# A fused attention and gated long convolution: last attention output through the DMA crossbar, biases by full-row products, smaller masks, another order

## Chip, cores and metric

The kernel runs on one core of a Trainium2 chip. The core has a matrix engine (PE, with its weight loads shown as PEld), a vector engine (DVE), an activation engine (ACT), GpSimd (POOL) and SyncE (SP); SP and POOL are used here mainly to issue DMAs. Every engine works through its own list of instructions in order, and waits there for semaphores of others. The metric is the device time of one execution in microseconds (us), the median of several runs.

## The reference

Four batches of eight heads, 768 positions, head size 64. The attention keeps, for each query, the eight first keys and the 96 keys up to itself, with a penalty that grows with distance, a slope for each head. Its output is the input `x` of a gated convolution over the whole sequence, done by Fourier transform.

```python
scores = scale * q @ k^T                                  # scale = 1/8
rel = pos[:, None] - pos[None, :]
is_global = pos[None, :] < 8;  is_local = (rel >= 0) & (rel < 96)
dist = where(is_global & ~is_local, 96, abs(rel))
scores = scores - slopes[h] * dist                        # slopes[h] = 2 ** -(h+1)
a = softmax(where(is_global | is_local, scores, -1e9));   o = a @ v
x = o.transpose(0, 2, 1, 3).reshape(4, 768, 512)
x1, x2, x3 = split(x @ w_proj, 3)                         # 512 -> 3 * 512
y = x1 * irfft(rfft(x2) * rfft(filter_fft)) * x3
out = y @ w_out                                           # float32, (4, 768, 512)
```

## The kernel before

**Attention.** Keys are cut into seven tiles `m` of 128 rows: the eight global keys first, then 120 keys of their own. A key tile meets 216 queries (168 and 48 in the last two). `attention(b)` works in three groups `c` of key tiles, (0, 1), (2, 3), (4, 5, 6). For each group, q and k tiles are transposed to `QT` and `KT` (by PE products with an identity, `turned`, or for batch 0's first tiles from f32, `turned32`; for batch 3 by transposing DMAs that SP issues, `crossed`). `scores` makes, for a pair of heads `hp`, two PSUM banks of 432 columns, ACT takes the exponential of both into `E` (L721), and DVE multiplies with `mask`, the exponential of the penalties (L738). In batch 0 there is no such product: the penalties are added to the scores in PSUM, by products of 64 rows with the tables `near` and `slope` (L698). `values` (L756, L761) multiplies with v and a column of ones, `rc` (L785) takes the reciprocal of the sums, and the product with it (L780) gives `xn`. `transpose_x` (L801) turns `xn` on PE, and a copy (L303) puts it into `xT`.

**Gates and convolution.** `gate` makes x1 and x3 for 384 positions at a time from `xT` (L840); x1 is scaled out of PSUM (L307, L309), x3 is copied out by ACT (L849) and multiplied by x1 on DVE (L851), or DVE takes x3 from PSUM in that product. `butterfly` adds and subtracts the halves and thirds of the sequence (L816 to L827); `conv` projects them (L909, evicted to `ab`), transforms (`forward`, L621, evicted to `X`), multiplies with the filter's spectrum (L1061 to L1078), transforms back (`inv`, L934, evicted to `eo`), joins the thirds and halves (`mixed`, `gated`; L1018 to L1041, the last one the product `y*g` with the gate), multiplies with `w_out` (L961), evicts to one of six tiles `ot` and stores.

**Tables.** In the beginning `setup`, `distances`, `masks`, `tables`, `inverse_tables` and `spectrum` make identities, penalties, masks, the Fourier matrices (from angles, with the sine on ACT), and the filter's spectrum.

**Loads.** SP brings four f32 tiles at first (`load_first32`); POOL issues all other loads of q, k, v, the weights and the filter, and casts them to 16 bit (L319). The first eight keys and values of a batch are copied to all tiles by further DMAs that SP issues (`kglobal`, `vglobal`).

**The order.** The program is a list of operations (`Plan.op`). Which engine does each, in which order, and in which PSUM banks, is written out in the text `ORDER`: `738V` is operation 738 on DVE, `31A` on ACT, `87P0` on PE into bank 0, G is POOL and S is SP. `i14b0` are 14 products of zeros into bank 0. An operation's number is its place in the order in which the functions list them. No cost decides anything at run time; the engines follow this list and their semaphores.

```python
n = next(i for i, x in enumerate(word) if x in "PAVGS")
o, at = self.ops[int(word[:n])], [int(x) for x in word[n + 1:]]
o.eng = word[n]
```

Of the kernel before, what the change touches and what calls it, by code (L numbers as in the profile page):

```python
# [16 lines left out]
P = 128  # L17
NG = 8
# [21 lines left out]
5G 33V 34A 1V 16S 0V 12V 20S 4V 41A 43A 9V 8V 39A 10A 44A 36A 6A 49A 48A 19S 37A 45A 24G 17S 18S 50G 55G 25V 11V 26G  # L40
13V 56G 40A 42A 7V i14b0 87P0 54G 28A 53G 60G 31A 85P1 61G 59G 27A 72V 62G 52G 35A 81P2 51G 57G 46A 58G 83P3 47A 88A
29V 30V 32V 90P0 63G 89A 86A 82V 38A 91V 84A 21V 114P2 115V 94P01 98P45 116P2 78A 65G 99A 64G 15V 117V 95A 92P67 112P3
113V 93A 110P2 96P45 97A 158P3 66G 111V 122P01 123A 120P67 121A 22V 68G 159V 3G 160P3 161V 14V 23S 156P2 118P45 162P3
67G 119A 124P01 261G 157V 163V 164P23 125A 166P45 100P01 165A 101V 102V 167A 105P67 170P23 171A 69G 168P01 169A 131P45
262G 263G 106V 107V 108P2 132V 133V 260G 126P67 127V 76A 103P3 104A 109V 128V 75A 134P4 221P5 74A 135V 172P01 73A 173V
259G 129P6 216P4 177P23 79A 130V 136P6 174V 175P7 178V 70G 146P0 217A 264S 179V 180P1 137P2 222A 223V 142P3 176A 218V
219V 71G 80A 271G 202V 181A 183P1 182P4 203V 220A 224V 209V 144A 141P5 210V 138A 211V 148V 205V 361P3 273G 225A 139V
140V 272G 270G 265S 188P7 185A 362A 212V 213V 151P6 266G 363P3 2A 153V 143A 364V 359P2 360V 152P6 228P3 154V 276G
365P01 190A 184V 77A 204V 279G 366A 206V 207V 371P45 198P2 277G 226V 367V 155V 297P7 368P01 214V 372A 373V 215V 208V
200A 374P45 187P6 278G 229A 274G 145V 491G 298A 288P2 375A 269G 275G 369A 289A 488G 286P7 227V 235V 236V 189V 237V  # L50
147P4 149V 238V 287A 150V 230A 231A 232A 233V 284P2 285A 312P7 292P6 313A 293A 389P5 387P2 192P7 390A 194A 193P6 195A
388V 394P45 395A 400P01 234V 391P23 392A 239V 240V 376V 299P7 300A 437P6 401A 301P4 302A 282G 268S 433P5 435P7 438V
281G 370V 397P23 398A 241V 249P6 250A 393V 434V 247P4 436V 402V 267S 382P01 494S 242P5 248A 448P67 243A 439P23 493S
440A 383V 384V 449A 396V 303P4 377P01 197P5 199A 304A 399V 408P23 441V 492G 244P6 378V 379V 305P5 409V 410V 380P4
445P01 245A 442P23 280G 381V 306A 196V 446A 450V 403P67 404V 443A 411P5 489G 587P4 499G 405V 256P01 412A 490G 385P6
257A 505G 386A 258A 591P7 588V 252P45 253A 254A 507G 406P0 447V 456P23 661P1 444V 508G 501G 662A 407V 414P0 589P4 590A
251V 307V 416A 310P5 311A 511G 290P6 424P1 457V 458V 291A 426A 459P0 423P4 425A 429P6 308V 431A 500G 451P23 665P1
418P6 255V 592A 191V 615P4 314V 315V 506G 718G 309V 322P7 452V 246A 460A 502G 420A 453V 186V 323A 617P5 719G 454P0
455A 295V 294V 296V 732G 666V 318P6 721S 413P7 616A 330P0 316P2 509G 481V 482V 484V 317A 326P1 618A 415A 663P4 428P2
201V 430V 319A 320P3 321V 324P5 483V 325A 331V 328P7 327A 419P6 329A 421V 422V 495G 472P2 730G 664A 283G 734G 466P7  # L60
432V 476P3 474A 497S 468A 599P45 735G 628P01 478V 600A 498G 529P2 332V 629A 485V 486V 530A 462P3 676P45 677A 333V 601V
673P01 674A 596P67 487V 516P2 597A 334V 464A 512P4 726G 513A 527P5 602P67 517V 717G 593P23 603A 630V 728G 619P01 620A
525P4 675V 514P6 528V 335V 336V 339V 504G 526A 622P01 496S 594A 625P45 626A 340V 477P7 621V 623A 479A 627V 598V 515A
503G 737G 427V 467P2 469A 350P3 670P01 739G 624V 667P45 671A 540P7 541A 604V 353P6 722S 716G 533P2 668A 733G 595V 337V
461P0 354A 520P7 470V 531P1 605P45 417V 606V 521A 729G 351A 818S 538P6 607V 534A 356P7 539A 817S 636P45 338V 463A 637V
532A 638V 631P23 632V 357A 633A 518P0 471P1 639P7 640A 519A 672V 473A 669V 678V 341P6 342A 888S 610P45 608P2 344P3
345A 542V 611V 612V 510G 684P45 890S 609V 480V 613P2 634P6 614A 536V 465V 523V 679P01 635A 685V 686A 347P7 535V 646P6
652P2 654A 656P3 731G 843S 680V 681V 543V 648A 682P4 736G 658A 475V 687P5 688A 651P2 815S 522V 524V 653A 544P3 552P6
545A 537V 720G 816S 819S 823P01 824A 683V 553A 709V 710V 723G 724S 725S 712V 829P45 554P3 711V 713V 555A 647P2 830A
738G 714V 657P0 659A 548P3 549A 556P6 715V 546P1 547A 845S 660V 558P4 559A 649A 557V 704P0 706V 550P1 348A 551A 642P3  # L70
644A 560V 561V 690P2 692A 844S 727G 842S 562V 849P67 852P01 846P45 641P3 563V 564V 740P2 853A 753P0 847A 741V 826P45
850A 643A 855P67 820P23 754A 827A 744P1 891S 831V 567V 565V 699P0 821A 757P4 745A 568V 742P1 856A 655V 758A 566V 889S
854V 895P67 701A 768P4 743A 755P5 857V 746P1 352S 756V 896A 769A 747A 748P0 645V 355S 898P67 828V 901P45 892P23 575P1
825V 899A 749A 851V 650V 902A 848V 705P6 707A 822V 897V 689P0 900V 837P45 349S 838V 839V 893A 751V 700P6 702A 576A
695P7 697A 858P23 859V 860V 832P45 894V 766P1 767A 691A 759P7 761P6 762A 903V 578P1 750V 343S 752V 840P6 833V 863P23
864V 865V 760A 694P7 834V 579A 909P01 910V 911V 841A 346S 770V 904P23 861P6 862A 866P4 771V 572P5 573A 835P6 569P0
836A 912P5 905V 906V 584P6 763V 570A 764V 765V 867A 772P0 773A 907P4 784P1 908A 913V 934V 935V 780P2 778P0 696A 779A
781A 884P3 774P7 786P0 580S 936V 886A 708V 787A 937V 782P2 938V 358S 585V 581P3 785A 577S 776P1 775A 883P7 777A 783A
788V 958P0 959V 939V 940V 879P2 941P6 698V 586S 942V 789A 790V 885A 873P0 791V 881A 954P1 955A 875A 956P2 693V 967P1
969P6 957A 945P0 868P2 703V 930P7 968A 870A 943P1 960P2 962P4 869P5 792V 795V 796V 944A 961A 812P2 793V 970A 794V 946A  # L80
947P6 871A 574S 963A 971V 972V 887V 949P5 878P4 813A 950A 948A 874P2 876A 582A 803P5 964V 965V 966V 992P2 979P6 952V
951V 988P3 583S 975P0 980A 877V 800P1 953V 990P6 976A 880V 993A 804V 986P2 801V 991V 987A 989A 814S 994V 872V 977P4
978A 882V 973P5 974A 981V 995A 571S 996V 997V 982V 983V 984V 915P0 985V 809P6 797P1 810A 920P6 922A 998V 798A 999V
811S 1000V 1001V 919P5 932A 929P4 806P1 1012V 799S 917A 914P0 1002V 807A 808S 925P7 921A 923V 931A 933V 916V 927A 805S
918V 1013V 924P5 1009P4 926A 802S 1003P5 1004A 1005S 1014V 1010A 1011S 1006P0 1007A 1008S 928V 1015V 1019P5 1020A
1021S 1022P4 1023A 1016P5 1024S 1017A 1018S
"""

# [110 lines left out]
class Fused:  # L199
# [428 lines left out]
    def turned32(self, what, o, t):  # L628
# [13 lines left out]
        if what == "k":  # L642
            self.global_keys()
# [580 lines left out]
```

## Time and profile before

| | |
|---|---|
| time, three runs | 178.73, 179.9, 180.12 us; median 179.9 us |
| span of the profiled execution, first to last instruction | 176.2 us |
| granted PE clock | 1.000 |
| DMA | 22.23 MB in 98188 packets |
| first exponential of scores (ACT L721) starts | 12.45 us |
| last product y*g (DVE L1041) starts | 169.59 us |
| last eviction (ACT L307) ends | 173.23 us |

The span is that of one execution; the time of a run holds what lies around it too. In the lines of a profile, an entry such as `E<-bank 128x864 f16<-128x864 f32 x48` is what is written, what is read, the shape (partitions x elements) and the number of instructions. A helper's line (L303 copies, L307 and L309 scalings, L319 loads) stands for many places; there the names tell the place.

### The profile page before, as it was taken

What the parts mean: (1) busy time and instruction counts of PE and PEld (TensorE: products, weight loads), DVE (VectorE), ACT (ScalarE), POOL (GpSimd) and SP (SyncE); (2) the same over time, 40 slices, a digit from 0 to 9 for tenths busy, and PEclk for the clock granted to TensorE, in tenths of its full rate; (3) what the DMA queues carried; (4) which work ended last, traced back from release to release, by engine and by line L of the source; (5) the groups of instructions that cost most, each with busy time, mean ns of one, the idle gap of its engine ahead of it and who ended that gap; (6) DMA issues with size and microseconds to landing.
All of it is one profiled execution on the core that took longest, in us unless ns stands there. A gap on an engine that the chain in (4) does not pass through costs nothing.

```text
span 176.2 us, 4332 instructions
## 1 busy us (share of the span) xinstructions
PE 163.8 (93%) x1662; PEld 100.3 (57%) x1662; DVE 156.3 (89%) x339; ACT 148.7 (84%) x294; POOL 78.2 (44%) x99
## 2 busy tenths in 40 slices
PE   5989999689999999999899999999999999989981
PEld 2547976354655767654356767444676644556530
DVE  7685569869999999999999999999999999999960
ACT  6999998949999988889989999899856855957852
POOL 7999998828999468799950000000000000000000
PEclk9999999999999999999999999999999999999999
DMA  4999999999999989999999995400031030041564
GB/s 110 184 149 140 142 173 170 196 193 154 159 155 159 149 53 106 156 167 155 130 161 169 131 96 159 179 4 0 0 118 65 0 125 0 0 180 40 192 242 186
DMA packets 98188, 22.23 MB, mean 126 GB/s; under 512 B 90879, under 2 KB 95095, under 8 KB 98167
## 3 DMA queue, kind: packets, MB, share of 16 engines
q0 software_dynamic: 82992, 12.41, 98.6%
q1 hardware_dynamic: 15175, 9.54, 23.1%
q8 instruction: 13, 0.21, 0.5%
q14 instruction: 8, 0.07, 0.1%
HBM read 25.84 MB, written 6.29 MB: 182 GB/s over the span
## 4 chain that ended last, share of the span: by engine, by line
DVE 48%; PE 15%; POOL 11%; ACT 11%; issue 7%; DMA 6%; POOLq 0%; DVEq 0%; ACTq 0%; SPq 0%
DVE E L738 6%; PE bank L961 4%; DMA kn<-in_k_dram 4%; DVE xn L780 4%; DVE y L1041 4%; POOL vn L319 4%; DVE g L851 3%; DVE y L1036 3%; PE bank L840 3%; ACT E L721 3%; POOL kn L319 2%; DVE ab L309 2%; POOL qn L319 2%; ACT g L849 2%; DVE pp L1072 2%
## 5 line engine op out<-in xcount | busy, mean ns | idle before, releaser
L840 PE MATMUL bank<-xT,w 128*128 128x384 f16 x256 | 48.5, 326 | 0.2 <-DVE x L309 0.2
L721 ACT ACTIVATE E<-bank 128x864 f16<-128x864 f32 x48 | 40.7, 900 | 4.1 <-issue 2.2
L840 PEld LDWEIGHTS <-w 128*128 128x128 f16 x256 | 23.7, 98 | 16.1 <-issue 1.4
L319 POOL DMA_DIRECT2D kn<-in_k_dram x27 | 25.1, 935 | 6.3 <-DMA g<-in_moe_filter_fft_dram 2.7
L319 POOL DMA_DIRECT2D vn<-in_v_dram x28 | 25.5, 917 | 0.8 <-PE bank L761 0.8
L961 PE MATMUL bank<-wo,y 128*128 128x512 f16 x96 | 23.9, 379 | 1.1 <-DVE y L1041 1.1
L319 POOL DMA_DIRECT2D qn<-in_q_dram x21 | 18.9, 905 | 4.0 <-PE bank L621 3.9
L738 DVE TENSOR_TENSOR E<-E,mask 128x864 f16<-128x864 f16 x36 | 20.2, 599 | 0.0
L780 DVE TENSOR_TENSOR xn<-bank,rc 128x512 f16<-128x512 f32 (+1 forms) x22 | 16.9, 774 | 0.7
L756 PE MATMUL bank<-vn,E 128*128 128x65 f16 x224 | 15.5, 193 | 0.2 <-DVE xn L780 0.2
L307 ACT ACTIVATE ot<-bank 128x512 f32<-128x512 f32 x21 | 12.6, 620 | 3.7 <-PE bank L961 3.3
L756 PEld LDWEIGHTS <-E 128*128 128x128 f16 x224 | 14.0, 97 | 2.8 <-issue 0.8
L303 ACT CAST eo<-bank 128x384 f16<-128x384 f32 x28 | 12.3, 496 | 3.8 <-PE bank L937 3.7
L761 PE MATMUL bank<-vn,E 128*128 128x65 f16 x192 | 15.3, 193 | 0.0
L707 PE MATMUL bank<-QT,KT 64*128 64x216 f16 (+2 forms) x224 | 14.4, 241 | 0.8 <-DVE ab L309 0.3
L849 ACT CAST g<-bank 128x384 f16<-128x384 f32 x28 | 13.9, 502 | 1.5 <-PE bank L840 1.2
L961 PEld LDWEIGHTS <-y 128*128 128x128 f16 x96 | 8.8, 98 | 10.1 <-DVE y L1041 2.2
L303 ACT CAST X<-bank 128x512 f16<-128x512 f32 x24 | 13.6, 607 | 0.7 <-PE bank L621 0.7
L761 PEld LDWEIGHTS <-E 128*128 128x128 f16 x192 | 13.2, 97 | 1.0 <-issue 0.8
L307 ACT ACTIVATE x<-bank 128x384 f16<-128x384 f32 x23 | 11.4, 509 | 1.8 <-PE bank L840 1.0
L707 PEld LDWEIGHTS <-KT 64*128 64x128 f16 x224 | 8.3, 94 | 7.5 <-issue 4.6
L934 PE MATMUL bank<-inv,X 128*128 128x256 f16 x64 | 11.4, 273 | 1.1 <-DVE X L1078 1.1
(148 smaller groups left out, 348.3 us busy)
## 6 DMA issues: line engine op xcount, KB each, us to landing
out_dram<-ot SPq DMA_DIRECT2D x24, 256.0 KB
vn<-in_v_dram POOLq DMA_DIRECT2D x28, 120.0 KB, 5.6
kn<-in_k_dram POOLq DMA_DIRECT2D x27, 120.0 KB, 5.8
qn<-in_q_dram POOLq DMA_DIRECT2D x21, 128.0 KB, 5.9
w<-in_moe_w_proj_dram POOLq DMA_DIRECT2D x4, 256.0 KB, 6.8
ot<-in_q_dram SPq DMA_DIRECT2D x3, 256.0 KB
g<-in_moe_filter_fft_dram POOLq DMA_DIRECT2D x1, 768.0 KB, 11.4
w<-in_moe_w_proj_dram POOLq DMA_DIRECT2D x1, 512.0 KB, 8.7
```

The costliest lines, as they stand in the source:

```text
L303: {"A": nc.scalar.copy, "V": nc.vector.tensor_copy, "G": nc.gpsimd.tensor_copy}[e](out, in_)
L307: self.nc.scalar.mul(out, in_, c)
L319: return self.g.op(eng, 0.57 + 0.00035 * nbytes[0] if eng == "G" else 0.5, lambda _: e.dma_start(dst, src), w=w, r=r, nbytes=nbytes, name= ...
L707: nc.tensor.matmul(bs[hh].f32()[:, off:off + w], self.KT[hs, hp, P * m:P * m + P], self.QT[hs, hp, KL * m:KL * m + w], start=(off == 0 and ...
L721: g.op("A", act(864), lambda _: nc.scalar.activation(eo, bs[0].two()[:, :, 0:432].rearrange("p h (m w) -> p h m w", m=2), Act.Exp, scale=s ...
L738: g.op("V", dve(864, 2), lambda _: nc.vector.tensor_mul(eo, eo, mk), r=[("mask", 2 * hp), ("mask", 2 * hp + 1)], w=[("E", hp, gi)], name=" ...
L756: nc.tensor.matmul(o[:, n, hh], ef[:, at:at + P], vt[:, t, 2 * hp + hh, 0:D + 1], start=first, stop=(t == 0), skip_group_check=True)
L761: nc.tensor.matmul(o[:, n, hh], ef[:, at:at + P], vt[:, t - 1, 2 * hp + hh, 0:D + 1], start=False, stop=True, skip_group_check=True)
L780: nc.vector.tensor_mul(to, o[:, :, :, 0:D], rc.to_broadcast([P, 2, 2 * nt, D]))
L840: nc.tensor.matmul(bk.f32()[:, 0:h], self.w[:, c, o + P * j:o + P * j + P], self.xT[:, c, h * s:h * s + h], start=(c == 0), stop=(c == 3))
L849: first = g.op("AV", {"A": act(h), "V": 0.0005}, lambda e: nc.scalar.copy(x3, pts[1].f32()[:, 0:h]) if e == "A" else None, use=[pts[1]], w ...
L961: nc.tensor.matmul(bk.f32(), y[:, c, P * t:P * t + P], self.wo[:, c, :], start=(c == 0), stop=(c == 3))
```

## The change

1. *Last batch's attention output.* For batch 3, `transpose_x` issues two transposing DMAs on SP for each call (12 in all) in place of PE transposes and a copy. `xT` gets a wider layout `xTt` of seven tiles of 128 columns (the last 8 of each are not used), so the gates of batch 3 take 360 and 408 positions, with one more product of 48 columns, and the butterfly's first two steps are three instructions each. The first half of `y*g` of batch 3 needs both halves of the gate.
2. *Biases of batch 0.* `near` holds the scaled penalties of each head, in 128 rows; one product with a 128x128 identity adds them, another the difference in the first and the last tile (`edge`). The 64-row tables and the 16 `slope` tiles are gone.
3. *Masks.* One exponential of 216 columns for each head; the other parts of `mask` are made from it on DVE (a product with `far`, a copy, a scaling with `tail`). They are listed after the first attention.
4. *First tiles.* SP loads k tile 1 and q tile 3 in f32 as well, six tiles; POOL no longer does.
5. *Spectrum.* The halving of the spectrum's first row moves into the table `twin` (`ends`); four one-row instructions are gone.
6. *Stores.* The last batch's last output tile is made and stored in two halves (`HALVES`).
7. *Order.* A new `ORDER`. Options for dense transforms (`DF`, `DI`) are added and left empty.

```diff
+    XX = (3,)
+    NEAR = True
+    HALVES = (5,)
+    DF = ()
+    DI = ()
...
-        for lo, hi in ((1, 2), (2, 7)):
+        for lo, hi in ((2, 7),):
...
+    def biases(self):
+        g, v = self.g, self.nc.vector
+        for h in range(8):
+            g.op("V", dve(216, 4), lambda _, h=h: v.tensor_scalar(
+                self.near[:, h], self.dg, self.slopes[h] / self.scale, None, op0=Alu.mult), r=["dg"],
+                w=[("near", h)], name="near")
...
+    def biased(self, hp, gi, bs):
...
+            for hh in range(2):
+                o, n = bs[hh].f32(), self.near[:, 2 * hp + hh]
+                kw = dict(stop=False, skip_group_check=True)
+                if gi < 2:
+                    mm(o[:, 0:432].rearrange("p (m w) -> p m w", m=2), self.identb,
+                       n[:, None, :].to_broadcast([P, 2, 216]), start=True, **kw)
+                    if gi == 0:
+                        mm(o[:, 0:KL], self.identb, self.edge[:, 0:KL], start=False, **kw)
+                    continue
+                for at, lo, w in ((0, 0, 216), (216, 0, 168), (384, 72, 48)):
+                    mm(o[:, at:at + w], self.identb, n[:, lo:lo + w], start=(at == 0), **kw)
+                mm(o[:, 384:432], self.identb, self.edge[:, KL:168], start=False, **kw)
...
         for h in range(8):
-            g.op("A", act(648), lambda _, h=h: nc.scalar.activation(
-                self.mask[:, h], wide, Act.Exp, scale=self.slopes[h]), r=["wide"],
+            g.op("A", act(n), lambda _, h=h: nc.scalar.activation(
+                mask[:, h, n:2 * n], self.dg, Act.Exp, scale=self.slopes[h]), r=["dg"],
                 w=[("mask", h)], table="exp", name="mask")
+        for hp in range(4):
+            hs = slice(2 * hp, 2 * hp + 2)
+            g.op("V", dve(2 * n, 2), lambda _, hs=hs: v.tensor_mul(
+                mask[:, hs, 0:n], mask[:, hs, n:2 * n], self.far[:, None, :].to_broadcast([P, 2, n])),
+                r=[("mask", 2 * hp), ("mask", 2 * hp + 1), "far"], w=[("mask0", hp)], name="mask0")
...
+        if self.b in self.XX:
+            for i in range(2):
+                g.op("S", 0.3 + 0.25 * len(ts), lambda _, i=i: nc.sync.dma_start_transpose(
+                    out=self.xTt[:, 2 * j + i, ts[0]:ts[-1] + 1],
+                    in_=self.xn[j][:, i, ts[0]:ts[-1] + 1].rearrange("p t h d -> p (t h d)")),
+                    r=[("xn", j, c)], w=[("xT", j, c, i)], nbytes=(32 * len(ts), 1024), name="crossx")
+            return
...
+                t = self.xTt[:, hs]
+                to = ab[:, x, :, 0:360].rearrange("p j (t r) -> p j t r", t=3)
+                fn(to[:, :, :, 0:96], t[:, :, 0:3, 0:96], t[:, :, 3:6, 24:KL])
+                fn(to[:, :, :, 96:KL], t[:, :, 0:3, 96:KL], t[:, :, 4:7, 0:24])
+                fn(ab[:, x, :, 360:h], t[:, :, 3, 0:24], t[:, :, 6, 24:48])
...
-                                    ("q", 2, self.q, 2, 0)):
+                                    ("k", 4, self.k, 1, NG), ("q", 2, self.q, 2, 0), ("q", 5, self.q, 3, 0)):
...
+            parts = 2 if last and t in self.HALVES else 1
...
+        if self.NEAR:
+            self.biases()
+            self.attention(0)
+            g.batch = (-10.0, 0.0)
+            self.masks()
```

The first and the last lines of the new `ORDER`, beside those of before:

```diff
-5G 33V 34A 1V 16S 0V 12V 20S 4V 41A 43A 9V 8V 39A 10A 44A 36A 6A 49A 48A 19S 37A 45A 24G 17S 18S 50G 55G 25V 11V 26G
+0V 8V 5V 9V 3G 230P0 18S 29V 6G 22S 10V 231A 232V 233V i1b1 225P1 14V 20S 15V 7A 11A 35G 19S 12V 37G 234A 61V 226A
+227V 21S 228V 70P2 i1b3 97P3 99P0 103P1 73P4 100V 17S 71A 72A 36G 41G 52G 13A 27G 98A 30G 229A 43G 104V 23S 28V 101P5
...
-1021S 1022P4 1023A 1016P5 1024S 1017A 1018S
+1016A 1012P7 1013V 1020S 1017S 1014S 1034P0 1035V 1036S 1028P6 1029V i1b1 1030S 1025P1 i1b4 2A 1026A 1027S 1031P4
+1032V 1033S
```

More of the change, by code (lines that the diff above doesn't have):

```diff
@@ L641, in turned32 @@
             w=[(what.upper() + "T", t)], name=what + "T")
-        if what == "k":
+        if what == "k" and t == 0:
             self.global_keys()
@@ L688, in scores @@
         m0 = self.GRP[gi]
+        if near:
+            self.biased(hp, gi, bs)
         def run(_):
             off = 0
-            if near:
-                runs = ([(0, 432)], [(216, 216), (216, 216)], [(216, 216), (216, 168), (432, 48)])[gi]
-                for at, w in runs:
-                    for k in range(2):
-                        for hh in range(2):
-                            hs = slice(64 * hh, 64 * hh + 64)
-                            nc.tensor.matmul(bs[hh].f32()[:, off:off + w], self.slope[hs, hp, k],
-                                             self.near[hs, k, at:at + w], start=(off == 0 and k == 0),
-                                             stop=False, skip_group_check=True)
-                    off += w
-                off = 0
             for m in m0:
@@ L871, in attention @@
                     self.turned32("k", 3, 0)
+                    self.turned32("k", 4, 1)
+                    continue
+                if b == 0 and c == 1 and what == "q":
+                    self.turned32("q", 5, 3)
                     ts = ts[1:]
@@ L875, in attention @@
             for i in range(4):
[L876 removed]
+                self.scores(i, c, self.NEAR and b == 0)
             for j in range(2):
@@ L1042, in gated @@
                                                                     gt[:, js, hs]),
-             r=ys + [("g", b % 2, j, half) for j in range(js.start, js.stop)], w=ys, name="y*g")
+             r=ys + [("g", b % 2, j, x) for j in range(js.start, js.stop) for x in ((0, 1) if half == 0 and b in self.XX else (half,))], w=ys, name="y*g")
     def spectra(self, b, pair):
```

433 lines of the change are left out of this document (262 added, 171 removed).

## The prediction

> **What bounds the kernel now.** First the page's busy times, then stretches of the span, to see which engine is full where, then the chain of waits for the start, and last the timeline and the groups for prices.
>
> ```profile
> PE 163.8 (93%) x1662; PEld 100.3 (57%) x1662; DVE 156.3 (89%) x339; ACT 148.7 (84%) x294; POOL 78.2 (44%) x99
> ```
>
> Three engines are nearly full, so no average names the bound. The stretches (columns: length, then PE, PEld, DVE, ACT, POOL busy, then clock, DMA share, GB/s):
>
> ```profile
> 12.45:20.00 7.55, 7.55 (x145) 5.86 (x145) 3.77 (x11) 7.35 (x10) 7.55 (x9) 1.00 2.24 142
> 20.00:30.00 10.00, 9.78 (x180) 7.44 (x177) 8.16 (x20) 9.25 (x16) 9.55 (x13) 1.00 1.68 165
> 30.00:40.00 10.00, 7.74 (x70) 4.68 (x68) 7.88 (x19) 7.72 (x14) 5.63 (x7) 1.00 1.65 191
> 40.00:105.00 65.00, 63.39 (x692) 39.58 (x691) 63.50 (x132) 61.87 (x125) 44.08 (x49) 1.00 2.00 140
> 105.00:165.00 60.00, 58.31 (x499) 34.64 (x498) 58.66 (x112) 46.79 (x93) 0.00 (x0) 1.00 0.20 70
> ```
>
> Before 20 us DVE is half empty; from 40 to 165 us it is full (122.16 of 125 us). In the second of those stretches ACT has 13 us free, so there DVE is the bound and ACT is not. From 30 to 40 all three have gaps. The chain of waits says why:
>
> ```profile
> 23.34 7.47 DMA kn<-in_k_dram
> 30.89 2.62 DMA kn<-kn
> ```
>
> POOL issues loads one behind another; batch 1's first key tile is issued only at 23.34, lands at 30.8, and its first eight keys are copied by a second DMA until 33.5. Only then do its scores begin.
>
> **Prices.** A row's length overlaps the next instruction, so the price is the distance between starts:
>
> ```profile
> 53.47 0.69 DVE L780 TENSOR_TENSOR xn<-bank,rc 128x512 f16<-128x512 f32 x1
> 54.08 1.64 DVE L738 TENSOR_TENSOR E<-E,mask 128x864 f16<-128x864 f16 x3
> 55.63 0.20 DVE L785 RECIPROCAL rc<-bank 128x8 f32<-128x8 f32 x1
> ```
>
> 0.61 for a 690 ns instruction and 0.52 each for three of 600: mean less 0.08 on DVE. On ACT four 738 ns exponentials take 2.64 in a row, a distance of 0.63, so mean less 0.11. The groups (columns: busy, mean ns of one, idle before) that most edits are priced by:
>
> ```profile
> L849 ACT CAST g<-bank 128x384 f16<-128x384 f32 x28 | 13.9, 502 | 1.5 <-PE bank L840 1.2
> ...
> L307 ACT ACTIVATE ab<-bank 128x512 f16<-128x512 f32 x18 | 11.0, 622 | 1.7 <-PE bank L909 1.5
> ...
> L851 DVE TENSOR_TENSOR g<-g,x 128x384 f16<-128x384 f16 x28 | 9.5, 352 | 0.1
> ...
> L545 ACT ACTIVATE mask<-mix 128x648 f16<-128x648 bf16 x8 | 5.6, 738 | 0.0
> ...
> L309 DVE TENSOR_SCALAR ab<-bank 128x512 f16<-128x512 f32 x6 | 4.1, 682 | 0.0
> ...
> L851 DVE TENSOR_TENSOR g<-bank,x 128x384 f16<-128x384 f32 x4 | 2.2, 550 | 0.0
> ```
>
> **The named edits.** *Masks:* eight exponentials of 648 columns become eight of 216. With 0.63 at 648 columns and 0.79 to 0.84 at 864 (two in 1.57 in the chain, ten in 8.41), 216 cost 0.2 to 0.3; I take 0.24, 8 x 0.39 = 3.1 us off ACT; four products, a copy and a scaling come onto DVE, 4 x 0.29 + 0.42 + 0.17 = 1.75. *Biases:* the 16 slope tiles (251 ns, distance 0.23) and three table copies leave ACT: 3.7 + 2.1 = 5.8 us, most of it before 9.4 us, when ACT waits for loads anyway. On DVE the old tables cost 4.5 (the tile for the masks 1.4, zeroing, copies) and the new ones about 2.8. The products themselves gain nothing:
>
> ```profile
> 11.03 0.54 PE L698 MATMUL bank<-eo 64*128 64x432 bf16 x4
> 11.50 0.36 PE L707 MATMUL bank<-QT,KT 64*128 64x216 f16 x4
> ```
>
> Four half-height products of 432 columns have a distance of 0.47, and two full-height pairs of 432 and 120 columns come to 0.46 at 0.42 ns a column (four L961 products of 512 columns: 0.86). *Crossbar:* 28 transposes of 128 columns at 0.056 (1.6 us) leave PE, and with them the six xT copies of batch 3, 5 x 0.5 on ACT and 0.36 on DVE. SP gets 12 transposing DMAs; those of now (L660, median 1.25 us on SP) move four 128-column blocks, these two or three. A crossed tile is later than a copied one: the nearest row, the small copy kn<-kn, takes 2.6 us, so I bound an xn-to-xT hop at 2.6 to 5.5 us (two issues in line, then landing), against about 1 now. Queued behind the crossings on SP are stores; an ot tile is written again only when its store has landed (0.3 us of such waits now), so a late store delays an ot eviction, for which only PSUM waits. What hides it: between the last xn of batch 3 and the butterfly that reads xT, DVE is given eight 0.6 us operations of batch 2 and one of 0.87, 5.7 us. Its cost is 0 to 2 on this path; I take 0. The butterfly's first two steps become three instructions each, +0.3. The Trainium skill, "DMA: Bandwidth & Descriptors", section "Anatomy of one DMA", speaks against small transfers: about 2.0 us fixed for each. By it a hop is at least 2.0 us, which the cover holds too.
>
> **The new order.** Decoding both lists by the order in which the operations are listed gives who does what. DVE: ab evictions 6 to 1 (-3.0), x1 9 to 3 (551 ns, so 0.47 each, -2.8), q copies 7 to 4 (-1.8), eo 4 to 2 (-0.9), the one-row fixes of the spectrum (four instructions, 1.3) replaced by two small ones (-1.15), xn 22 to 21 (-0.6); against that 12 more gates multiply from PSUM (+0.2 each, +2.4) and smaller moves. All together, by these prices, DVE 153.7 to 146.8 us and ACT 138.2 to 130.6. PE goes from 151.8 (3.0 of it the 14 dummy products) to 149.1 (1.3 dummies). On PE, price means streaming time; the page's 163.8 counts the drain too.
>
> **The start.** SP now brings six f32 tiles, not four (k1 and q3 leave POOL), and the filter goes from place 31 to 7 on POOL, ahead of eleven tiles; the Fourier angles and the filter's sums run in the empty first 20 us. PE has tile q0, the last of the six, ahead of all scores. Now four SP tiles and some POOL tiles landed by 9.1 us, about 1 us a tile from 2.2; six and four give 12 to 13, so the first exponential at about 13 (12.45 now), with 12 and 17 as ends (17: the filter, 3.9 us by the distance of its landing, 39.6, from the one before it, 35.7, goes ahead too). DVE's own work ahead of its first reciprocal is 17.4 us (13.7 now), because filter work is pulled ahead; with the wait for bias tables I get 21.3 (20.1 now). Batch 1's first key is issued at about 19, not 23.3, so the gap at 30 to 40 closes. Weight slices w0 and w2 land later (28 and 33 by POOL's 0.92 a tile, 24.5 and 26.5 now); their first gates come at 35, so nothing. The last-batch key k1 stays next to last on POOL and should land at 85, its scores being due near 90.
>
> **The sum.** Two columns. DVE: from first reciprocal (20.13) to last y*g (170.13) are 150.0 us for 140.0 of work; after, 21.3 + 127.5 + the same 10.0 = 158.8, and with the end of now (6.1 us of last projections, store) a span of 164.9. PE: from the first values product (19.48) to the last projection (172.5) are 153 us for 139.0 of work, so 14 us of gaps; with 136.2 of work from 20 and the same gaps, 170.2, plus 3.7 to the end, 173.9. The gaps are mostly waits for DVE, and so shrink, but not by all of DVE's 12.5 us: I take the middle, 169.4. The profiled span of 176.2 stands 3.7 below the median of 179.9, so 173.1 us, called 173.
>
> The end gains little: the last tile goes out in halves (-0.25), two dummy products and a late Sin warm-up stand before the last evictions, whose table load (1.28 in this trace) fits into ACT's wait for PE.
>
> **Rivals.** *Tensor column holds:* PE's gaps stay as they are, since they come from PSUM banks and pipeline and not from DVE. 173.9 + 3.7 = 177.6, and up to 180.6 if the crossbar hop or a load shows by 3. For it: PE's 97% in the long stretches; against it: DVE is equally full there. Chance 0.15; one third of it below 178.1. *Late start (slower):* the chain's first 20 us are a queue of loads. If q0 lands at 17 and all behind it moves 5 us, with PE's gaps kept, 177.6 + 5 = 182.6. It decides at a first exponential later than 16.5 (181.7 in time). For it: 1 us a tile and the filter's place; against: SP's tiles are issued first. Chance 0.15. *Crossbar stalls the last batch:* if twelve crossings at 1.9 us (the longest L660 row) hold SP 23 us, the butterfly waits 6: 179. Chance 0.08, five of them within 1%. *Cold clock:*
>
> ```profile
> 1.78 5.83 PE L299 MATMUL bank<-idle 128*128 128x512 f16 x14 [1.78 <-DVE idle L368]
> ```
>
> The 14 dummies ran at 0.42 each and not at the 0.216 of later ones, and all behind them at full speed. The change leaves four scattered ones, so the first scores may run at half speed: at most 5.8 us of dense work, 2.9 us late, 176 in all; chance 0.1, inside the forecast. The Trainium skill, "TensorE: Matmul & The Clock Gate", part 1, has this rule (half clock until about 3.4 us of sustained work); by its figure the price would be 1.7. *Nothing but work hidden anyway:* if ACT and DVE only trade places, it is the first rival again.
>
> **Numbers.** Forecast 0.55, from 168.6 (DVE column) to 177.6 (PE column). Better than 168.6, DVE's 10 us gaps closing too: 0.07. 1% is about what a measurement of this kernel can tell (178.7 to 180.1 in three runs). Faster 0.55 + 0.07 + 0.05 = 0.67; same 0.10 + 0.05 = 0.15; slower 0.15 + 0.03 = 0.18. The range that leaves 0.2 out: 167 to 181.5.
>
> **What would show it.** Right: DVE busy near 149, ACT near 141; first exponential near 13, first reciprocal near 21; no empty stretch at 30 to 40; batch 3's scores near 90; DVE's idle before the last butterfly under 1 us. Wrong: first exponential past 16; PE waiting for a crossed xT; PE's gaps still 14 us; SP's line late.

## The result, and the profile after

The changed kernel takes 184.84 us (median of four runs, 184.22 to 185.68); the kernel before, on the same chip in between, takes 179.31 (178.02 to 180.12). The ratio is 1.0315, with a 95% interval of 1.025 to 1.038: slower by 3%, where 173.0 and faster was forecast, and outside the range of 167 to 181.5. The profiled execution took 184.27 us, its span is 182.3. Medians hold all runs; the ratios here and below leave out runs that took over 1.5% longer than the shortest of the same kernel, and the traces of `filter_later`, `q0_behind`, `cross_by_need`, `keys_early_q0`, `keys_early_q0_filter` and `cover_mid` are of such runs.

First the page, busy times and slices of 4.56 us each, as far as they are needed:

```profile
PE 161.5 (89%) x1622; PEld 102.2 (56%) x1622; DVE 149.7 (82%) x333; ACT 143.7 (79%) x281; POOL 76.0 (42%) x95
...
PE   5574999999979999999993199999996999999992
...
PEclk9999999999999999999999659999999999999999
DMA  6999999999999999999999920100233433303665
```

The work fell as forecast (DVE 149.7 for "near 149", ACT 143.7 for "near 141"), and the span grew by 6.1 us. The place is to be seen at once: slices 22 and 23 (96 to 105 us), where PE falls to 3 and 1, and the clock to 6 and 5 in slices 23 and 24. Up to there the DMA row stands at 9.

The stretches of the prediction, now of the changed kernel (columns: length, then PE, PEld, DVE, ACT, POOL busy, then clock, DMA share, GB/s):

```profile
12.45:20.00 7.55, 4.85 (x44) 3.15 (x42) 4.06 (x18) 3.05 (x6) 4.59 (x6) 1.00 1.69 177
20.00:30.00 10.00, 10.00 (x191) 7.85 (x188) 9.03 (x24) 9.96 (x16) 8.57 (x11) 1.00 2.19 164
30.00:40.00 10.00, 10.00 (x120) 6.78 (x117) 9.47 (x23) 8.96 (x22) 8.50 (x10) 1.00 2.05 171
40.00:105.00 65.00, 57.11 (x669) 37.67 (x666) 54.63 (x115) 53.97 (x99) 42.85 (x48) 0.98 2.07 143
105.00:165.00 60.00, 58.20 (x497) 35.27 (x494) 53.39 (x101) 48.17 (x108) 0.00 (x0) 0.97 0.22 64
```

The gap of before at 30 to 40 is closed. The start is emptier than it was (ACT 3.05 us, 7.35 before), and between 40 and 105 PE, DVE and ACT are each idle for 8 to 11 us, where they had been idle for 1.5 to 3.

The chain of waits of the changed kernel says for what (start, length, what):

```profile
5.00 12.52 DMA ot<-in_q_dram
...
90.87 0.46 SPq L748
91.38 1.78 SPq L748
93.26 2.97 SPq L748
96.32 2.46 SPq L748
98.83 5.06 DMA KT<-kn
103.94 1.26 PE bank L786 x12
...
137.46 3.99 DMA xT<-xn
```

The first line is SP's f32 load of q0. L748 is the transposing DMA that turns q and k tiles of batch 3 (`crossed`). Three of them (of q0, k4 and k1), 1.8 to 3.0 us each, stand in line on SP ahead of key tile k0's, and that one lands 5.06 us after its issue at 98.83. PE begins batch 3's first scores at 103.94. The waits of the changed kernel between 97 and 110 us (total, times, longest):

```profile
ACT E L798 <- PE bank L786: 6.8, 1, 6.8
PE bank L786 <- DMA KT<-kn: 6.7, 1, 6.7
```

And its stretches there, the wait itself and the work behind it:

```profile
97.00:104.00 7.00, 0.28 (x4) 0.07 (x4) 2.50 (x4) 0.74 (x2) 0.00 (x0) 0.85 1.62 148
104.00:108.40 4.40, 4.40 (x31) 2.92 (x32) 0.42 (x2) 2.80 (x4) 0.00 (x0) 0.50 0.38 49
```

Behind 6.7 us of waiting come 4.8 us of work at half the granted clock, from 103.94 to 108.72 (the second stretch shows 4.4 of them), by estimate 2.4 us lost again: 9.1 us in all. This is called the hole from here on.

### The profile page after: what moved, and what is told of

Read it like the earlier page. It is cut to its first block, busy times and chain, and to the rows that moved or that the text cites. A ratio compares the mean times of both kernels' runs of the same rounds, so it can differ in the third digit from the quotient of the medians.

```text
span 182.3 us, 4259 instructions
## 1 busy us (share of the span) xinstructions
PE 161.5 (89%) x1622; PEld 102.2 (56%) x1622; DVE 149.7 (82%) x333; ACT 143.7 (79%) x281; POOL 76.0 (42%) x95
## 4 chain that ended last, share of the span: by engine, by line
PE 64%; DMA 15%; SPq 6%; POOL 6%; ACT 4%; issue 2%; DVE 1%; POOLq 0%; DVEq 0%
PE bank L939 16%; PE bank L1080 10%; DMA ot<-in_q_dram 7%; PE bank L1018 6%; PE bank L786 6%; PE bank L941 5%; PE bank L1046 5%; SPq L748 4%; POOL qn L330 3%; DMA qn<-in_q_dram 3%; DMA KT<-kn 3%; PE bank L709 3%; PE bank L760 3%; ACT xn L862 2%; DMA xT<-xn 2%; SPq L330 2%
## 5 line engine op out<-in xcount | busy, mean ns | idle before, releaser
L939 PE MATMUL bank<-xT,w 128*128 128x384 f16 x192 | 37.8, 334 | 0.0
L330 POOL DMA_DIRECT2D kn<-in_k_dram x26 | 23.8, 924 | 0.8 <-issue 0.3
L939 PEld LDWEIGHTS <-w 128*128 128x128 f16 x192 | 17.7, 100 | 11.4 <-issue 1.6
L1080 PE MATMUL bank<-wo,y 128*128 128x512 f16 (+1 forms) x100 | 23.5, 370 | 0.0
L786 PE MATMUL bank<-QT,KT 64*128 64x216 f16 (+2 forms) x224 | 13.2, 248 | 6.7 <-DMA KT<-kn 6.7
L318 ACT ACTIVATE x<-bank 128x384 f16<-128x384 f32 (+2 forms) x29 | 14.2, 512 | 4.1 <-PE bank L939 1.4
L858 DVE TENSOR_TENSOR xn<-bank,rc 128x512 f16<-128x512 f32 (+1 forms) x21 | 16.2, 774 | 0.4
L314 ACT CAST eo<-bank 128x384 f16<-128x384 f32 x30 | 13.7, 503 | 3.1 <-PE bank L1049 2.5
L318 ACT ACTIVATE ab<-bank 128x512 f16<-128x512 f32 x23 | 13.7, 626 | 2.6 <-PE bank L1018 2.5
L941 PE MATMUL bank<-xT,w 128*128 128x360 f16 x64 | 12.4, 315 | 1.8 <-DMA xT<-xn 1.8
```

The source lines that it names most:

```text
L314: {"A": nc.scalar.copy, "V": nc.vector.tensor_copy, "G": nc.gpsimd.tensor_copy}[e](out, in_)
L318: self.nc.scalar.mul(out, in_, c)
L330: return self.g.op(eng, 0.57 + 0.00035 * nbytes[0] if eng == "G" else 0.5, lambda _: e.dma_start(dst, src), w=w, r=r, nbytes=nbytes, name= ...
L786: nc.tensor.matmul(bs[hh].f32()[:, off:off + w], self.KT[hs, hp, P * m:P * m + P], self.QT[hs, hp, KL * m:KL * m + w], start=(off == 0 and ...
L858: nc.vector.tensor_mul(to, o[:, :, :, 0:D], rc.to_broadcast([P, 2, 2 * nt, D]))
L939: nc.tensor.matmul(bk.f32()[:, 0:h], w, self.xT[:, c, lo:lo + h], **kw)
```

## The experiments

All are the changed kernel with one edit, `no_v3_before` excepted. Names: `k0` is key tile 0, all of batch 3 unless said; an order is given by its words decoded. In the tables, "first scores" is when PE starts batch 3's.

**The start.** Of two repairs, `filter_later` moves the 768 KB filter load on POOL, and DVE's work on it, behind batch 0's keys; `q0_behind` lets PE do three head pairs that need no q0 ahead of tile q0, the last of the six f32 tiles to land (17.5 us).

```diff
 POOL (filter_later)
-... ld filter (place 7) ... k4 b0, ..., k5 b0
+... k4 b0, ..., k5 b0, ld filter
 PE (q0_behind)
-tr32 q0 ... scores of three head pairs, group c1
+scores of three head pairs, group c1 ... tr32 q0
```

> The filter's load (768 KB) is issued behind the last k load of batch 0 instead of ahead of dg, and the first three operations of its spectrum stand behind the last key copy on VectorE; nothing else moves. If the filter in front of the first tiles makes the late start: q0, which landed at 17.5, lands by 14, the first exponential goes from 18.61 to about 15, and the time falls by 2 to 4 us from 184.8. If the six float32 tiles on SP's own queue make it: q0 still lands after 16.5 and the time stays within 1 us. If the lost time is only in the empty stretch at 95 to 108, the start moves and the time does not.

> No load moves. On TensorE the transposes of q0, on VectorE its copy, and on ScalarE the copy of vfirst stand behind the scores and exponentials of three head pairs of group 1, which need neither. If what was late is q0 and vfirst and only the order made everything else wait for them: the first exponential is at about 15.4 instead of 18.61, some 2.4 us of exponentials are done when q0 lands at 17.5, the first reciprocal is at 24 to 25 instead of 26.65, and the time falls by 2 to 3 us. If the start's lag is swallowed by the stretch at 95 to 108: 0 to 1 us. If q0 alone bounds the first values whatever goes ahead of it: first reciprocal within 0.5 us of 26.65 and no gain.

Measured: 185.95 us (184.15 to 188.4, four runs), ratio 1.0317 [1.0209, 1.0425], and 184.64 (183.69 to 189.96, five), 1.0298 [1.0188, 1.0407]. The first exponential came at 16.18 and 15.53 in place of 18.61, but DVE's first reciprocal at 27.01 and 28.32 in place of 26.65, and the first scores of batch 3 at 106.96 and 105.04. An earlier first score is not an earlier end here: what was gained at 16 was waited away before 28, and again at 97.

**The new crossings undone.** `xT_by_PE` turns batch 3's `xn` on PE again, with copies on ACT.

```diff
-    XX = (3,)
+    XX = ()
```

> Batch 3's attention output is transposed on TensorE again: 28 transposes and six copies on ScalarE in place of 12 crossings on SP (and the gate's halves of 384 columns go with it). If the crossings of the output cost what the trace shows: TensorE's wait of 1.80 us before the gates at 141.5 goes, 1.6 us of transposes and about 3.5 us of copies on ScalarE come in, and the time moves by -1.5 to +1 us. If the crossbar hop is the main loss: the time falls by 3 us or more. If it was hidden as forecast: it rises by 1 to 2 us.

Measured: 188.9 us (186.15 to 189.3, four), 1.0492 [1.0343, 1.064], slower than either expectation; first scores at 104.09. The twelve new transposing DMAs are not the loss. In the changed kernel their cost is in the waits between 110 and 150 us:

```profile
PE bank L941 <- DMA xT<-xn: 1.8, 1, 1.8
DVE xab L908 <- DMA xT<-xn: 1.7, 1, 1.7
```

**Which tile is late.** `cross_by_need` issues the crossings in the order in which the scores need them; `keys_early_only` brings k1, q0 and k2 ahead on POOL (before batch 2's last loads, with four v tiles moved back to wo) and leaves the crossings; `keys_early_need` does both; the two others add `q0_behind` and then the filter's move.

```diff
 SP, crossings of batch 3 (cross_by_need)
-q4 k6 q1 q2 k2 k5 q0 k4 k1 k0 q3 k3 q5
+q4 q1 q2 k0 q0 k1 q3 k3 k2 k6 k5 k4 q5
 POOL (keys_early_only)
-v2 ... v5 ... v1 ... k2 q0 v6 q5 k1 wo v3 v4
+k1 q0 k2 ... q5 v2 v5 v1 v6 wo v3 v4
```

> Only the order of batch 3's 13 crossings of q and k on SP changes: the five that the first scores read (q1, q2, k0, q0, k1) stand second to sixth, where q0 was seventh, k1 ninth and k0 tenth. If the order of the crossings makes the empty stretch at 95 to 108 (each takes 1.2 to 3 us on SP, so the tenth lands at 103.9): batch 3's first scores go from 103.9 to 92 to 95, TensorE's busy time in 95 to 105 rises from 3.3 us to over 6, and the time falls by 4 to 7 us. If the pace of the queue sets it whatever the order: the last group's scores still come at 105 or later and the time falls by 1 to 3. If the late start alone makes it: no change.

> The changed kernel with the same loads earlier and the crossings in its own order (k0 tenth). If both the order of loads and that of crossings count: first scores of batch 3 at 99 to 102 and 181 to 184 us, as k0's crossing is still tenth behind 1.2 to 3 us each. If the loads alone make it: as keys_early_need, within 1 us.

> cross_by_need with POOL's order of the last loads changed too: k1, q0 and k2 of batch 3 are issued some twelve loads earlier, v2, v5, v1 and v6 of batch 3 behind them. If k1's load (issued 83.44, landed 95.95 in cross_by_need) is what held the crossings there: no crossing waits for a load, five crossings at the 1.2 to 1.4 us of the trace from 80.5 on put batch 3's first scores at 88 to 92 instead of 102.4, the empty stretch 95 to 105 (TensorE 5.65 us of 10 in cross_by_need) fills to over 9, and the time is 175 to 178. If the crossings share the DMA engines with the loads and take 2.5 to 3 us each whatever is ahead: first scores at 95 to 97, time 178 to 180. If the late start bounds all: 181 or more.

> keys_early_need with the start of q0_behind. q0_behind alone moved the first scores from 18.2 to 15.1 and won nothing, as the stretch at 95 to 105 took it up. If the start counts as soon as that stretch is gone: 2 to 3 us under keys_early_need. If the crossings' own chain (scores of batch 2 leave QT and KT at 80) still takes it up: within 1 us of it.

> keys_early_q0 with the filter's load behind the last k load, as in filter_later, where the first scores came at 15.8 but the loads of v then stood behind the filter and TensorE and ScalarE stood idle at 25 to 30 (3.25 and 1.79 us busy of 5). If that idle only moved the start's loss: within 1 us of keys_early_q0. If the earlier q0 is worth its time: 2 us less. If the idle stretch with its granted clock of 0.82 to 0.84 costs more: 2 us more.

| | median (range, runs) | ratio [95%] | first scores | PE busy 95 to 110, of 15 |
|---|---|---|---|---|
| changed kernel | 184.84 (184.22 to 185.68, 4) | 1.0315 [1.025, 1.038] | 103.94 | 8.28 |
| cross_by_need | 182.32 (178.65 to 183.5, 4) | none formed | 100.88 | 10.65 |
| keys_early_only | 187.38 (185.41 to 187.82, 4) | 1.0503 [1.0412, 1.0593] | 105.35 | 7.75 |
| keys_early_need | 183.23 (181.7 to 184.41, 4) | 1.0286 [1.019, 1.0382] | 100.71 | 11.35 |
| keys_early_q0 | 181.86 (178.74 to 184.68, 10) | 1.0063 [1.0002, 1.0124] | 99.41 | 11.75 |
| keys_early_q0_filter | 184.15 (181.26 to 185.24, 4) | 1.0244 [1.011, 1.0378] | 103.19 | 11.27 |

Each of these was to close the hole by bringing the tile that PE waited for. In no trace did it close: the wait moved to the next tile. (In the four kernels that cross by need only two products start at the time of the table, and the next ten 1.1 to 1.5 us later.) Some of the loss came back in part of the runs: the ten runs of `keys_early_q0` spread from 178.74 to 184.68, and its ratio, 1.0063, is below the changed kernel's 1.0315; its trace is of a run of 181.72, so that what the shorter ones did is not seen. The chain of `cross_by_need`:

```profile
83.44 12.51 DMA kn<-in_k_dram
95.96 6.38 DMA KT<-kn
```

A 120 KB key tile takes 12.51 us from issue to landing and its crossing 6.38 more. With k1 fetched early (`keys_early_need`) its crossing alone, issued at 89.84, takes 11.89. So it isn't one tile or one place in the order: loads and crossings in general are slow at 83 to 104 us.

**Cover.** If the crossings are simply late, work moved ahead of batch 3's attention should cover them. `cover_short`, `cover_mid` and `cover_long` move 41, 51 and 96 operations of other batches ahead of 20, 25 and 45 of batch 3's attention; `cover_mid_q0` adds `q0_behind`.

```diff
 ORDER, places 639 to 700 (715, 780)
-b3 attention and other work in turns
+the other work, then b3 attention, each in the order that it had
```

> The changed kernel; only the written order moves, no load and no crossing. In the stretch of the order between batch 3's first scores and its scores of group 2, the 41 operations that are not batch 3's attention (transposes, gates, spectra and outputs of batches 0 to 2) stand ahead of the 20 that are. If the crossings' data come at 102 to 104 whatever the order (a full DMA), and what the change lost is the work that covered them: TensorE's busy time in 95 to 105 rises from 3.3 to 7 us or more, the granted clock there is over 0.9, and the time falls by 3 to 5 us. If VectorE or the bank evacuations then hold the moved work up: less than 2 us.

> As cover_short with a longer stretch: 51 operations, some 9 us of TensorE by the trace's durations (8 gates at 0.65, 3 outputs and 2 spectra at 0.43 to 0.87, two groups of transposes), ahead of 25 of batch 3's attention. By the theory of the lost cover: TensorE 8.5 us or more of 10 in 95 to 105, clock 0.95 or more, time 176 to 180. By the rival that the start is what is missing: 183 or more.

> As cover_mid, up to the projections of batch 2: 96 operations ahead of 45, which is more than the empty stretch holds. By the theory of the lost cover batch 3's scores then come later than their data (107 to 112) and the time is as cover_mid's or up to 3 us above it, since batch 3's own chain to the end starts later. If the end is set by the sum of work alone: as cover_mid or below.

> cover_mid with q0_behind's start (first scores at 15.1 instead of 18.2). If the crossings' data at 102 to 104 pace the middle and the moved work just fills the stretch: within 1 us of cover_mid. If the start's 3 us count once the stretch is filled: 2 to 3 us under it, 174 to 177.

Measured: 183.03 (182.16 to 183.97), 186.62 (183.68 to 187.78), 192.21 (191.63 to 192.74) and 186.26 us (184.46 to 187.03), four runs each; ratios 1.025 [1.019, 1.031], 1.0353 [1.0245, 1.0462], 1.0762 [1.0717, 1.0807] and 1.0402 [1.0317, 1.0488]. The stretches of `cover_short`:

```profile
97.00:104.00 7.00, 6.61 (x45) 3.72 (x44) 7.00 (x13) 3.80 (x9) 0.00 (x0) 1.00 1.66 116
104.00:119.00 15.00, 10.89 (x85) 5.57 (x84) 8.05 (x13) 11.08 (x16) 0.00 (x0) 0.77 0.35 53
```

The hole is filled (6.61 of 7 us), and a like one opens behind it, where the changed kernel's PE was full (15.00 of 15): the work moved ahead is missing between batch 3's exponentials, which ACT makes one after another. PE waits there for banks that ACT has not yet emptied:

```profile
PE bank L785 <- ACT E L797: 3.6, 3, 1.8
```

The more is moved, the longer the time. Filling the hole with work of other batches did not by itself bring the time back.

**Fewer bytes.** `no_v3` leaves out batch 3's seven loads of v (its products take batch 1's v, so that the output differs), 0.86 MB on POOL's queue; `no_v3_before` does the same to the kernel before.

```diff
+        if what == ("vn", 1) and b == 3:
+            return self.g.op("G", 0.0, lambda _: None, w=[what + (t,)], name="none")
```

> The changed kernel without batch 3's seven loads of v (its output product takes batch 1's v): order, crossings and all else as they were. If the volume in the DMA engines holds the crossings' data: k0's crossing lands at 94 to 98 instead of 103.9, the empty stretch shrinks by 6 to 8 us and the time falls to 177 to 180. If SP's pace of 13 crossings in 25 us is its own: first scores at 102 or later and the time within 1 us of 184.8.

> The same seven loads left out of the kernel before. Its first scores of batch 3 come at 105.2, but TensorE and VectorE are 4.9 to 5 us busy of every 5 there. If that is because its order holds other work for the wait: the time stays within 1 us of before. If it too waits for the data: 2 us or more below.

Measured: `no_v3` 175.78 us (175.13 to 176.76, four), 0.9866 [0.9816, 0.9917]; `no_v3_before` 178.71 (177.91 to 180.78, ten), 1.0025 [0.9994, 1.0055]. In the changed kernel seven loads less are worth 9.06 us by the medians (184.84 to 175.78), and some 8.0 by the ratios, which compare each with the kernel before on its own chip (1.0315 less 0.9866, of 178.3 us); the hole is 9.1. In the kernel before they are worth nothing. (Without them k1 is also issued 3.9 us earlier, at 78.83; by `keys_early_need` an earlier k1 alone does not close the hole.) The stretches of `no_v3`:

```profile
97.00:104.00 7.00, 7.00 (x66) 4.03 (x62) 6.99 (x13) 6.96 (x12) 0.00 (x0) 1.00 0.37 57
104.00:108.40 4.40, 4.40 (x49) 2.40 (x46) 4.37 (x8) 4.40 (x9) 0.00 (x0) 1.00 0.18 63
```

Full, at full clock, with a DMA share of 0.37 where it was 1.62. A crossing of a key tile holds SP for 1.24 us in the median here, for 2.46 in the changed kernel, and for 1.26 in the kernel before (ns, least, median and most; `no_v3`, changed, before):

```profile
L750 SPq DMA_TRANSPOSE KT<-kn x7: 1189/1241/1920, 80.9 to 96.8; - x7
L748 SPq DMA_TRANSPOSE KT<-kn x7: 1227/2461/2967, 81.4 to 101.5; - x7
L660 SPq DMA_TRANSPOSE KT<-kn x7: 1188/1258/1879, 82.9 to 105.3; - x7
```

So a full DMA row alone doesn't make the crossings slow. In the kernel before it is as full until 106 us:

```profile
DMA  4999999999999989999999995400031030041564
```

Its key loads issued between 70 and 100 us land within 6.2 us, against 12.2 in the changed kernel. Why they are quicker there was not tried. The load of `wo` (512 KB) is issued at 70.44 there and at 83.61 in the changed kernel; but it alone doesn't make the hole, as `no_v3` and, below, `v_last` issue it at 79.75 and 80.95 and have none.

That the kernel before doesn't notice the seven loads is no matter of an earlier start of batch 3: its first scores of batch 3 begin at 105.2, later than the changed kernel's 103.94. But it has other work until then: its values of batch 2 end at 100.4, with output products, transposes, gates and inverse transforms behind them, where the changed kernel has done with batch 2's values at 95.1 and asks for batch 3 at 97.2. From 97 us to the end, the stretch of the kernel before, and then of the changed one:

```profile
97.00:190.00 93.00, 73.38 (x641) 43.41 (x636) 71.60 (x143) 60.11 (x127) 0.00 (x0) 1.00 0.32 81
```

```profile
97.00:190.00 93.00, 73.28 (x592) 43.11 (x590) 67.90 (x135) 59.95 (x129) 0.00 (x0) 0.96 0.37 92
```

PE has nearly the same busy time left, 73.4 and 73.3 us (by the estimate above, 2.4 of the second are the half clock's). The old order has some 8 us of it placed ahead of batch 3's first scores, the new one next to nothing (0.28).

**The same bytes, later.** `v_late` puts `wo` and batch 3's v loads from v1 on behind k1's crossing, `v_last` those v loads behind all thirteen, each with `cross_by_need` and k1, q0, k2 early. A one-element copy on POOL that reads the last crossed tile makes POOL's queue wait there. The whole computation is done. Two more runs add `q0_behind`.

```diff
 POOL (v_last)
-v2 ... v5 ... v1 ... k2 q0 v6 q5 k1 wo v3 v4
+k1 q0 k2 ... q5 wo (copy below) v1 v2 v3 v4 v5 v6
+self.nc.gpsimd.tensor_copy(self.one[:, 0:1], self.QT[0:1, 0, 5 * P:5 * P + 1])
```

> Whole computation. POOL issues k1, q0 and k2 of batch 3 early (as keys_early_need), crossings by need, and wo and six of batch 3's v loads only once k1's crossing has landed (one copied element on POOL waits for it). By the theory of the volume: the first five crossings at 1.3 us each from 80.5, first scores at 90 to 94, time 176 to 180; wo then lands near 97 and may hold the first outputs of batch 0 by up to 2 us. By SP's own pace: first scores at 98 or later, no gain over cross_by_need.

> v_late with q0_behind's start. If the start's 3 us were only hidden by the full DMA: 2 to 3 us below v_late, 174 to 177, below the kernel before. If batch 2's scores, and with them the crossings' start at 80, do not move with the start: within 1 us of v_late.

> Whole computation. As v_late, but wo is loaded with the others (it lands near 90) and six of batch 3's v loads wait for the last crossing, q5's. By the theory of the volume: first scores of batch 3 at 90 to 94, the last crossing lands by 100, no stretch of 5 us with TensorE under 4 between 95 and 110, v lands at 101 to 112 beside the exponentials, and the time is 175 to 178.5: the 5 us that the change lost come back. If the values of batch 3 then wait for v: 179 to 182.

> v_last with q0_behind's start. First exponential at 15 instead of 18.5, but in all runs so far the first reciprocal stayed at 26.7 to 28.6 with it and without, so within 1 us of v_last; if the earlier exponentials count once the DMA no longer paces the middle: 2 us below.

| | median (range, runs) | ratio [95%] | first scores | PE busy 95 to 110, of 15 |
|---|---|---|---|---|
| v_late | 182.73 (181.08 to 183.84, 4) | 1.0221 [1.0142, 1.0299] | 97.17 | 11.17 |
| v_late_q0 | 181.6 (179.76 to 183.05, 4) | 1.0159 [1.0061, 1.0258] | 97.58 | 11.01 |
| v_last | 175.95 (174.06 to 182.18, 12) | 0.9814 [0.9763, 0.9865] | 97.90 | 15.00 |
| v_last_q0 | 175.17 (174.22 to 176.8, 6) | 0.9807 [0.9746, 0.9867] | 97.29 | 15.00 |

`v_late` came only half way: behind k1's crossing the loads ran into the rest, and q5's crossing took 8.70 us from 101.54. Both were expected to start batch 3's scores at 90 to 94 and started them at 97 to 98, although k1's crossing had landed by 90.8 in `v_late` (POOL's copy behind it runs then): by the order, batch 2's values come first and end at 95.1. `v_last` has no hole; its stretches:

```profile
97.00:104.00 7.00, 7.00 (x64) 4.11 (x63) 7.00 (x13) 7.00 (x13) 0.00 (x0) 1.00 0.54 100
104.00:108.40 4.40, 4.40 (x39) 2.41 (x37) 4.40 (x8) 4.40 (x8) 3.56 (x5) 1.00 0.64 93
```

It moves the same bytes on the same queues as the changed kernel, but for the one copied element, and is 4.8% shorter (175.95 / 184.84), and by its ratio 1.9% shorter than the kernel before. The times from issue to landing of the key loads between 70 and 100 us, first in the changed kernel, then in `v_last`:

```profile
DMA to landing us min/median/max: 4.4/5.4/12.2
```

```profile
DMA to landing us min/median/max: 4.8/4.8/5.4
```

These are not quite like with like: `v_last` has issued its last key load by 79.15, ahead of the crossings, the changed kernel at 82.71. A load of q0 that `v_last` issues at 80.04 still takes 8.65 us.

## Why the prediction was wrong

**The step that failed** is "The last-batch key k1 stays next to last on POOL and should land at 85, its scores being due near 90". It looked at when POOL issues a tile and took the landing for granted, and no term of the sum stood for the line of q and k crossings on SP. k1's load was issued here, and landed 12.2 us later, at 94.9:

```profile
82.71 0.99 POOL L330 DMA_DIRECT2D kn<-in_k_dram  x1
```

SP's line of crossings was slow too: SP came to k1's crossing at 96.32, 1.4 us behind the tile, and to k0's at 98.83, whose landing at 103.9 ended PE's wait. Crossings took 5 to 12 us from issue to landing in the traces above. "SP's line late", one of the prediction's signs of being wrong, is what came. The scores were due when batch 2's attention was done (97.2 here, 96.7 to 97.9 in the kernels without a hole, so "near 90" was early by 7 too) and met tiles of 104.

What takes the hole away is shown: to leave out v loads (`no_v3`), or to hold six of them back behind the crossings (`v_last`). That the new order also leaves no other work there is a second condition only by comparison with the kernel before, which starts batch 3's scores at 105.2 and is full until then; the `cover` runs, which put work there, lost time behind it, so that no run shows this condition by itself.

The Trainium skill, "DMA: Bandwidth & Descriptors", section "Issuing engines are not separate DMA queues", says it: DMAs that SP and GpSimd start run on the same 16 engines and interleave, so that another issuing engine saves issue time alone. The traces agree: SP's crossings are slow while POOL's loads stand in line, 2.46 us of issue for 1.24.

**The sum** of the forecast's DVE column, term by term, in us of span:

| | forecast | changed | no_v3 | v_last |
|---|---|---|---|---|
| first reciprocal starts | 21.3 | 26.65 | 26.88 | 28.76 |
| from there to the end of the last y*g | 137.5 | 148.61 | 139.38 | 138.23 |
| to the end of the span | 6.1 | 7.04 | 7.04 | 7.01 |
| span | 164.9 | 182.3 | 173.3 | 174.0 |

The middle term held within 2 us wherever the hole was closed: the prices of masks, biases, moves and gaps were right as a sum, though not each was measured by itself. In the changed kernel it has 9.23 us more than in `no_v3`, the hole (9.1 by the stretches). What is left, 1.88, is near DVE's wait for a crossed `xT`, 2.4 us in `no_v3`.

**The start** was the second miss. "the first exponential at about 13" came at 18.61, since q0, the sixth of SP's f32 tiles, was issued at 5.00 and landed 12.52 us later. This is the *late start* rival (first exponential past 16.5, slower), and even its 182.6 us is near the time, by luck, for it is not what decided: `v_last`, whose first reciprocal is 2.1 us later still, is faster than the kernel before. The 5.35 us by which the first reciprocal is late are read from the trace; no run recovered them, as moving q0 and the filter brought earlier scores and no earlier reciprocal. Whether they cost a full 5.35 at the end is open.

**The columns.** With the hole gone the span comes to 173.3 and 174.0, near the forecast's PE column (173.9) and not the middle that was taken (169.4). In part that is luck: the column lets the values' products begin at about 20 and keeps PE's gaps, while in `v_last` the first reciprocal, which follows such products, comes at 28.76, and PE is busy for 143.2 of the 145 us from 20 to 165 (139.2 before), so that its gaps shrank. The DVE column with its middle term kept and the late start put in comes to 170.5 for `no_v3` (26.88 + 137.5 + 6.1). That PE is the bound from 20 us on is what the profile of `v_last` shows; the *tensor column* rival's reason, banks and pipeline, was not tried.

**Crossed xT.** "Its cost is 0 to 2 on this path; I take 0": it is 1.8 on PE and 1.7 on DVE, at one place; a hop took 3.99 us, inside 2.6 to 5.5. The upper end was the better value. The rival by which the crossings of `xT` stall the last batch by 6 us fell.

**Prices that held**, by groups of the changed kernel (busy, mean ns of one, idle before):

```profile
L318 ACT ACTIVATE ab<-bank 128x512 f16<-128x512 f32 x23 | 13.7, 626 | 2.6 <-PE bank L1018 2.5
...
L955 DVE TENSOR_TENSOR g<-bank,x 128x384 f16<-128x384 f32 (+1 forms) x16 | 8.5, 544 | 0.3 <-issue 0.3
...
L953 ACT CAST g<-bank 128x384 f16<-128x384 f32 (+2 forms) x16 | 8.0, 509 | 0.1
...
L602 ACT ACTIVATE mask<-dg 128x216 f16<-128x216 bf16 x8 | 3.0, 391 | 0.0
```

Masks of 216 columns take 391 ns each, 0.28 by the rule of mean less 0.11 (0.24 was taken). Twelve gates went from ACT's copies to products from PSUM, 28 to 16 and 4 to 16. "Weight slices w0 and w2 land later … so nothing" held: 30 to 40 us is full.

**Cold clock.** In the changed kernel's trace fewer dummy products did not slow the first scores (clock 1.00 at 12.45 to 30). In others the clock fell there, behind the wait for q0: `v_last` has 0.86 at 20 to 30. In the changed kernel it fell in the hole, in a place that the rival hadn't named.

Not tried: undoing masks or biases alone, or the old order with the new code, as an order is written for one list of operations.

## What to carry to other kernels

When an order is made tighter, look for the tiles that it now needs first, and price their landing by the longest landing of such a tile while the DMA row stands at 9 (11.3 us for a key tile in the kernel before, where the median was 5.8), not by the time of their issue. This price is a suggestion; no forecast was made with it. Where loads and crossings are slow and a tile is needed, bringing that tile earlier or reordering its crossing moved the wait to the next tile in every trace here; what closed the hole, with the whole computation done, was to hold loads that weren't due yet back behind the crossings, though they stand on another queue. And before work is moved into a gap, see what it covered where it stood: here that is read off the kernel before, not shown by a run.

## What the hardware showed beside this

The granted clock of PE fell to 0.50 at 101.9, 4.7 us into the 6.7 us wait, and stayed there until 108.72, through 4.8 us of dense work. The Trainium skill, "TensorE: Matmul & The Clock Gate", part 1, gives half clock behind an idle window of about 3.4 us and full clock after about as long of sustained work. The fall agrees with that; the 4.8 us are longer. Shorter waits at the start do not sort by length: 2.70 us of PE idle in the changed kernel left the clock at 1.00, 3.21 in `v_last` brought 0.50 from about 19.4 to 22.8, and only 1.85 in `cross_by_need` brought 0.50 from about 19.1 to 22.5. By that page's window 1.85 us would not be enough; the measurement decides, and what else counts was not settled.

One 120 KB load lands in 4.4 to 12.2 us within the same 30 us of one run, and a transposing DMA of one tile holds its issuing engine for 1.2 us or for 3.0. With such a spread a single duration from a trace is no price of a DMA.
